# Chunked attention and two feed-forward layers on one core: seven block products on three PSUM banks per group, and another rule for GpSimd's share

## The chip, the cores and the metric

The kernel runs on one core of one Trainium2 chip. The engines are TensorE (PE, with its weight loads as PEld), VectorE (DVE), ScalarE (ACT), GpSimd (POOL) and SyncE (SP), which issues the DMAs. The metric is the time of one execution in microseconds, the median over runs on the device.

## The reference

Three steps follow each other on 3072 tokens (4 sequences of 768):

```python
# attention in chunks of 32 queries; 8 memory keys, 16 left, 8 right
a = softmax(q_c @ concat(mem_k, k_ctx).T / 8); out_c = a @ concat(mem_v, v_ctx)
x = out as (3072, 512)
h = np.maximum(x @ w_in, 0.0);  x = h * h @ w_out               # 512 -> 2048 -> 512
g = x @ w_gate;  silu = g * (1.0 / (1.0 + np.exp(-g)))
return (silu * (x @ w_val)) @ w_out2                            # 512 -> 1536 -> 512
```

Everything is float32 in and out. The weights come in as 64-bit words and are turned into float32 by the kernel itself.

## The kernel before

The tokens are six blocks of 512. Every matrix product is made of three products of high and low parts (`TERMS`), so each operand is split first: ACT writes the high part (`split`, line 414), DVE or POOL subtracts it to get the low part (line 421).

**First part.** Attention of all blocks and the first feed-forward layer of blocks 0 to 3 are done directly, with 2048 hidden columns in 16 steps (`first_layer`, line 668; `first_out`, line 696).

**Second part.** The last two blocks of the first layer and all three pairs of blocks of the second layer are done with 2-by-2 blocks and seven products in place of eight (the Strassen and Winograd scheme). A left side is a group of weights; its sums and differences are prepared by `sides` and kept in DRAM (L830, L379 to L402, L432 on `f` and `g` tiles), and come back by `load_in` or `load_out`. The right sides are sums of blocks of the activations, made and split by `rights` into tiles `r` and `x`. `group` (line 891) issues one product of 6 matmuls of 128x512 into a PSUM bank. `first_quad` runs seven products for each of 8 groups, and `second_gate` seven for each of 12 groups in each of three pairs, which makes 44 groups. After each product ACT copies the bank out (`copy`, line 441), or DVE adds it to a tile (`sub` on `FROM`, line 432); what is left is combined from tile to tile by `sub` with the costs `DIFF`, on DVE or POOL. `out_layer` (line 1001) does the way back in seven products over all groups, four times, each with two banks per product.

In a group the products come as 1, 5, 6, 2, 7, 3, 4. Product 2 is added onto the bank of 1 and product 3 onto that of 5, after ACT has copied those out; 6, 7 and 4 have a bank each, so a group uses five of the eight banks.

**The order.** Nothing of the order is written by hand. Each step is an `Op` with a cost for every engine that may do it, and `Plan.run` (a list scheduler) puts the ops on the engines in the order of their ranks; PE may look ahead over a few products. An op that DVE and POOL can both do goes to an engine only if the other would not end it sooner. The instructions are then issued in this fixed order, so each engine works through its own queue, and an instruction that waits holds up all that stand behind it. Pools of tiles: `PS` 8 banks, `T2` 5 tiles for what leaves the banks, `U` the blocks, `R` and `X` the split operands.

Of the kernel before, what the change touches and what calls it, by code (L numbers as in the profile page):

```python
# [39 lines left out]
HI, LO = 0, 1  # L40
# [10 lines left out]
QUAD = (1, 5, 6, 2, 7, 3, 4)  # L51
# [9 lines left out]
DUE = 12.0  # L61

# [11 lines left out]
class Op:  # L74
    __slots__ = (
        "engs", "fn", "deps", "succ", "bufs", "new", "n", "start", "end", "ready", "asap",
        "rank", "tail", "move", "eng", "soon", "at",
    )


class Plan:
# [9 lines left out]
    def op(self, engs, fn, reads=(), writes=(), tail=0.0, move=0.0):  # L91

        o = Op()
        o.engs, o.fn, o.tail, o.move, o.at = engs, fn, tail, move, self.due
        o.n, o.succ, o.start, o.eng, o.soon = len(self.ops), [], None, None, self.soon
# [57 lines left out]
    def run(self, pools, slack=12.0, ahead=8, phases=(), gives=None):  # L153
# [48 lines left out]
        def place(o, e):  # L202
# [6 lines left out]
            engines[e] = t + o.engs[e]  # L209
# [87 lines left out]
DIFF = {"DVE": 0.72, "POOL": 1.35}  # L297
# [7 lines left out]
def tile_chunked_attention_two_ffn(ctx: ExitStack, tc, qd, kd, vd, w1, w2, wo2, out):  # L305
# [45 lines left out]
    def words(src, token=None):  # L351
# [8 lines left out]
        def word(n):  # L360
# [17 lines left out]
            {"DVE": 0.5},  # L378
# [3 lines left out]
            (), (a,),  # L382
        )
        pl.op(
            {"DVE": 0.5},
# [4 lines left out]
            (), (a,),  # L390
        )
        pl.op(
            {"DVE": 0.8},
# [4 lines left out]
            (raw,), (a,),  # L398
        )
        pl.op(  # L400
            {"DVE": 0.8},
# [3 lines left out]
            (t,), (a,),  # L405
# [3 lines left out]
    def split(dst, src, reads, keys, n=512, diff=None):  # L409
# [9 lines left out]
        def low(e):  # L419
# [4 lines left out]
            costs, low, list(reads) + [(b, (q, HI)) for b, q in keys], [(b, (q, LO)) for b, q in keys]  # L424
        )

    def sub(out, x, y, op=ALU.subtract, engs=None):
# [5 lines left out]

        return pl.op(engs or DIFF, run, (x[0], y[0]), (out[0],))

# [9 lines left out]
    def whole(b):  # L445
        return (b, lambda: at(b))
# [17 lines left out]
    class Unit:  # L464
# [158 lines left out]
        def leave(self, xb, a):  # L623
# [6 lines left out]
                diff={"DVE": 0.69},  # L630
# [216 lines left out]
    def rights(b11, b12, b21, b22, name):  # L847
# [4 lines left out]
        yield 2, hilo(name, b21)  # L852
# [3 lines left out]
        sub(b11, b22, b11)  # L856
        yield 6, hilo(name, b11)
        sub(b21, b11, b21)
# [40 lines left out]
    FROM = {"DVE": 0.69}  # L899

    def first_quad(w, r):

        bank, pl.soon = {}, True
        a = pl.buf("T2", "a")
        b11, b12, b21, b22 = (pl.buf("U", n) for n in ("b11", "b12", "b21", "b22"))

        def product(i, onto=None):
            bank[i] = bank[onto] if onto else pl.buf("PS", f"p{i}")
            group(bank[i], w, i, r, onto is None)

        def squared(b):
            def run(e):
                if e == "ACT":
                    nc.scalar.activation(out=at(b), in_=at(b), func=AF.Relu)
                    nc.scalar.activation(out=at(b), in_=at(b), func=AF.Square)
# [349 lines left out]
```

## Time and profile before

| | |
|---|---|
| median of 3 runs | 1196.51 us (1194.54 to 1199.16) |
| profiled execution | 1196.86 us |
| its span, first to last instruction | 1194.8 us |
| PE busy | 1109.7 us (93%) |
| DVE busy | 994.5 us (83%), 1563 instructions |
| ACT busy | 604.6 us (51%), 1257 instructions |
| POOL busy | 473.9 us (40%), 353 instructions |
| mean granted TensorE clock | 0.977 of 2.4 GHz |

The profiled execution takes 2.1 us more than its span. Busy shares are averages over stages with different limits: the first 450 us hold the attention and the direct products, 463 to 612 us the eight groups of the first layer, and from about 612 us on the three pairs of the second layer follow. A time "for" another engine in a view of waits is the idle time that this engine's semaphore ended.

### The profile page before, as it was taken

What the parts mean: (1) busy time and instruction counts of PE and PEld (TensorE: products, weight loads), DVE (VectorE), ACT (ScalarE), POOL (GpSimd) and SP (SyncE); (2) the same over time, 40 slices, a digit from 0 to 9 for tenths busy, and PEclk for the clock granted to TensorE, in tenths of its full rate; (3) what the DMA queues carried; (4) which work ended last, traced back from release to release, by engine and by line L of the source; (5) the groups of instructions that cost most, each with busy time, mean ns of one, the idle gap of its engine ahead of it and who ended that gap; (6) DMA issues with size and microseconds to landing.
All of it is one profiled execution on the core that took longest, in us unless ns stands there. A gap on an engine that the chain in (4) does not pass through costs nothing.

```text
span 1194.8 us, 17679 instructions
## 1 busy us (share of the span) xinstructions
PE 1109.7 (93%) x6044; PEld 901.6 (75%) x6044; DVE 994.5 (83%) x1563; ACT 604.6 (51%) x1257; POOL 473.9 (40%) x353
## 2 busy tenths in 40 slices
PE   5898999999999997989799999669999999999998
PEld 5666788778877876868578887458888888888887
DVE  6999988888798886799997799998566998567992
ACT  5877756656656664556644344534122454223450
POOL 0324546666243344177822235881000571001640
PEclk9999999999999998999899999889999999999999
DMA  9664477778868688857599986665955365954462
GB/s 351 214 225 163 142 262 278 278 263 284 292 237 306 234 290 291 306 185 275 185 360 342 376 304 208 222 212 170 399 198 185 92 225 182 349 192 159 152 195 76
DMA packets 100073, 288.48 MB, mean 241 GB/s; under 512 B 10768, under 2 KB 14864, under 8 KB 99984
## 3 DMA queue, kind: packets, MB, share of 16 engines
q1 hardware_dynamic: 99984, 287.35, 68.7%
q8 instruction: 48, 0.79, 0.3%
q14 instruction: 41, 0.34, 0.1%
HBM read 210.24 MB, written 77.07 MB: 240 GB/s over the span
## 4 chain that ended last, share of the span: by engine, by line
PE 51%; DVE 24%; DMA 8%; issue 8%; ACT 5%; POOL 2%; SPq 0%; DVEq 0%; POOLq 0%; ACTq 0%
PE ps L891 28%; PE ps L1001 13%; PE ps L668 4%; PE ps L696 4%; DVE u L432 3%; DMA g<-in_w 3%; DVE g L421 3%; DVE a L568 3%; DVE r L421 3%; DVE f L394 2%; DVE f L432 2%; DVE t L432 1%; ACT t L524 1%; DVE f L402 1%; DVE f L379 1%
## 5 line engine op out<-in xcount | busy, mean ns | idle before, releaser
L891 PE MATMUL ps<-r,r 128*128 128x512 f32 x981 | 242.8, 390 | 3.8 <-ACT a L441 2.0
L891 PEld LDWEIGHTS ps<-r,r 128*128 128x128 f32 x981 | 184.4, 188 | 43.0 <-ACT a L441 2.4
L668 PE MATMUL ps<-x,r 128*128 128x512 f32 x768 | 190.0, 396 | 6.3 <-DVE r L421 4.4
L441 ACT ACTIVATE t<-ps 128x512 f32<-128x512 f32 x165 | 98.2, 596 | 153.3 <-PE ps L891 111.7
L668 PEld LDWEIGHTS ps<-x,r 128*128 128x128 f32 x768 | 142.2, 189 | 39.7 <-DVE r L421 5.6
L1001 PE MATMUL ps<-r,r 128*128 128x512 f32 x600 | 150.8, 402 | 17.4 <-ACT f L441 11.6
L891 PE MATMUL ps<-r,x 128*128 128x512 f32 x579 | 147.4, 394 | 5.7 <-ACT t L441 5.7
L1001 PEld LDWEIGHTS ps<-r,r 128*128 128x128 f32 x600 | 116.3, 195 | 44.5 <-ACT f L441 13.2
L696 PE MATMUL ps<-r,w 128*128 128x512 f32 x552 | 138.5, 401 | 12.0 <-POOL r L421 3.6
L696 PEld LDWEIGHTS ps<-r,w 128*128 128x128 f32 x552 | 104.9, 192 | 37.6 <-POOL w L421 4.0
L891 PEld LDWEIGHTS ps<-r,x 128*128 128x128 f32 x579 | 110.4, 191 | 29.8 <-ACT t L441 6.6
L414 ACT ACTIVATE g<-f 128x512 fp32r<-128x512 f32 (+1 forms) x136 | 76.9, 578 | 72.8 <-DVE f L394 26.7
L414 ACT ACTIVATE r<-u 128x512 fp32r<-128x512 f32 x126 | 75.2, 624 | 61.4 <-DVE u L432 29.1
L421 DVE TENSOR_TENSOR g<-f,g 128x512 fp32r<-128x512 f32 (+1 forms) x103 | 94.1, 923 | 7.9 <-ACT g L414 7.0
L421 POOL TENSOR_TENSOR r<-u,r 128x512 fp32r<-128x512 f32 x36 | 58.0, 1618 | 100.0 <-ACT r L414 87.4
L432 DVE TENSOR_TENSOR t<-t,ps 128x512 f32<-128x512 f32 x80 | 54.6, 683 | 48.1 <-PE ps L891 38.1
L421 POOL TENSOR_TENSOR r<-t,r 128x512 fp32r<-128x512 f32 x32 | 50.1, 1564 | 107.4 <-ACT r L414 99.7
L421 DVE TENSOR_TENSOR r<-u,r 128x512 fp32r<-128x512 f32 x90 | 79.6, 910 | 7.4 <-ACT r L414 6.6
L568 DVE STREAM_TRANSPOSE a<-t 32x128 f32<-32x128 f32 x256 | 77.4, 302 | 7.0 <-POOL t L552 2.8
L432 POOL TENSOR_TENSOR f<-f,f 128x256 f32<-128x256 f32 (+1 forms) x38 | 35.1, 924 | 113.0 <-DVE f L432 69.4
L432 POOL TENSOR_TENSOR u<-u,u 128x512 f32<-128x512 f32 x38 | 61.2, 1619 | 45.2 <-DVE u L432 22.1
L441 ACT ACTIVATE t<-t 128x512 f32<-128x512 f32 x36 | 22.7, 631 | 101.3 <-DVE t L432 101.3
(124 smaller groups left out, 2002.3 us busy)
## 6 DMA issues: line engine op xcount, KB each, us to landing
r<-tma SPq DMA_DIRECT2D x71, 512.0 KB, 5.2
g<-in_w SPq DMA_DIRECT2D x56, 512.0 KB, 4.8
r<-tmb SPq DMA_DIRECT2D x50, 512.0 KB, 3.6
x<-tma SPq DMA_DIRECT2D x37, 512.0 KB, 4.8
tma<-g SPq DMA_DIRECT2D x36, 512.0 KB, 3.7
tlb<-g SPq DMA_DIRECT2D x56, 256.0 KB, 3.4
tla<-g SPq DMA_DIRECT2D x24, 512.0 KB, 3.9
tmb<-g SPq DMA_DIRECT2D x42, 256.0 KB, 3.2
```

The source lines that it names most:

```text
L379: lambda: nc.vector.tensor_scalar(out=at(a), in0=at(a), scalar1=EXP_MIN, scalar2=EXP_MAX, op0=ALU.max, op1=ALU.min),
L394: lambda: nc.vector.scalar_tensor_tensor(out=at(a).bitcast(I32), in0=word(1), scalar=-0x40000000, in1=at(a).bitcast(I32), op0=ALU.bitwise_ ...
L402: lambda: nc.vector.tensor_tensor(out=at(a).bitcast(I32), in0=at(a).bitcast(I32), in1=at(t).bitcast(I32), op=ALU.add),
L414: lambda: nc.scalar.activation(out=dst(HI), in_=src(), func=AF.Copy),
L421: eng.tensor_tensor(out=dst(LO), in0=src(), in1=dst(HI).bitcast(F32), op=ALU.subtract)
L432: eng.tensor_tensor(out=out[1](), in0=x[1](), in1=y[1](), op=op)
L441: nc.scalar.activation(out=out[1](), in_=x[1](), func=func)
L568: nc.vector.transpose(out=o[g : g + 32, hh, :, :, m, :].rearrange("k s (f c) q -> k s f c q", c=2)[:, :, :, par, :], in_=a[r : r + 32, :, ...
L668: nc.tensor.matmul(at(hp), at(w)[:, 512 * a + k * P : 512 * a + (k + 1) * P], x[:, b, k, :], start=(n == 0), stop=(n == len(terms) - 1),)
L696: nc.tensor.matmul(at(accs[m]), at(w)[:, 512 * a + m * P : 512 * a + (m + 1) * P], at(h2)[:, 512 * b : 512 * b + 512], start=(i == 0 and n ...
L891: nc.tensor.matmul(at(bank), at(w[slot])[:, o : o + P], at(r[i, n])[:, 512 * b : 512 * b + 512], start=(first and n == 0 and m == 0), stop ...
L1001: nc.tensor.matmul(at(bank[i][n]), at(w[i][g // 2])[:, o : o + P], at(r)[:, 512 * b : 512 * b + 512], start=(first and m == 0), stop=(g == ...
```

## The change

The scheme of seven products is arranged in another way. Three banks serve a group: 1, 6, 7 and 4 are added one after the other onto the first, 5 and 3 onto the second, 2 has the third. The bank is read after each product, so what it holds is already a running sum, and tile-to-tile additions fall away. A new function `quads` issues the products: 1 and 5 of a group, then product 4 of the group before, then 6, 3, 2, 7. `out_layer` does the same with order 1, 5, 6, 3, 7, 2, 4. `rights` makes the same seven sums with one sign turned.

The scheduler has a new rule for POOL. Ops with all operands in SBUF are marked `shared`; if such an op starts on DVE while POOL is at work, its cost grows by `SLOWED` of the overlap. POOL takes an op only if it would be `AVOID` sooner than DVE. Some DVE costs are lowered to 0.45, 0.69 and 0.7.

```diff
+SLOWED, AVOID = 0.55, 0.3
...
-            engines[e] = t + o.engs[e]
+            cost = o.engs[e]
+            if e == "DVE" and o.shared:
+                cost += SLOWED * max(0.0, min(cost, engines["POOL"] - t))
+            engines[e] = t + cost
...
-                            x != e and busy(x, o.rank) + o.engs[x] < t + o.engs[e] for x in o.engs
+                            x != e and busy(x, o.rank) + o.engs[x] < t + o.engs[e] + (e == "POOL") * AVOID
+                            for x in o.engs
...
-DIFF = {"DVE": 0.72, "POOL": 1.35}
+DIFF = {"DVE": 0.69, "POOL": 1.3}
+FROM = {"DVE": 0.69}
...
+    def quads(lefts, r, begin):
+        last = None
+        for n, left in enumerate(lefts):
+            w, a, b, c = left(), *(pl.buf("PS", x) for x in "abc")
+            steps = begin(n)
+
+            def product(i, w=w, steps=steps, a=a, b=b, c=c):
+                bank = {1: a, 6: a, 7: a, 4: a, 5: b, 3: b, 2: c}[i]
+                pl.soon = True
+                group(bank, w, i, r, i in (1, 5, 2))
+                steps[i](bank)
+                pl.soon = False
+
+            product(1)
+            product(5)
+            if last:
+                last(4)
+            for i in (6, 3, 2, 7):
+                product(i)
+            last = product
+        last(4)
...
-    def second_gate(w, r):
...
-        product(6)
-        sub(whole(a), whole(a), whole(bank[6]), ALU.add, FROM)
-        product(2, 1)
-        copy(whole(d), whole(bank[1]), func=AF.Sigmoid)
-        sub(whole(d), whole(bank[1]), whole(d), ALU.mult, FROM)
-        product(7)
-        sub(whole(b), whole(a), whole(bank[7]), ALU.add, FROM)
-        sub(whole(c), whole(b), whole(c), ALU.add)
-        product(3, 5)
-        sub(whole(a), whole(a), whole(bank[5]), ALU.add, FROM)
-        copy(whole(e), whole(a), func=AF.Sigmoid, engs=C512)
-        sub(whole(e), whole(e), whole(a), ALU.mult)
-        sub(whole(c), whole(c), whole(e), ALU.mult)
-        product(4)
-        sub(whole(b), whole(b), whole(bank[4]), ALU.subtract, FROM)
-        sub(whole(b), whole(b), whole(d), ALU.mult)
...
+    def second_quads(left, r):
...
+            def third(k):
+                sub(whole(e), whole(e), whole(k), ALU.add, FROM)
+                copy(whole(f), whole(e), func=AF.Sigmoid, engs=C512)
+                sub(whole(f), whole(f), whole(e), ALU.mult)
+
+            def second(k):
+                sub(whole(a), whole(a), whole(k), ALU.add, FROM)
+                copy(whole(d), whole(a), func=AF.Sigmoid, engs=C512)
+                sub(whole(d), whole(d), whole(a), ALU.mult)
+
+            def seventh(k):
+                sub(whole(c), whole(k), whole(c), ALU.add, FROM)
+                sub(whole(c), whole(c), whole(f), ALU.mult)
+
+            return {
+                1: lambda k: copy(whole(a), whole(k)),
+                5: lambda k: copy(whole(c), whole(k)),
+                6: lambda k: copy(whole(e), whole(k)),
+                3: third, 2: second, 7: seventh,
+                4: lambda k: sub(whole(b), whole(k), whole(d), ALU.mult, FROM),
+            }
...
-        order = (1, 5, 2, 3, 7, 6, 4)
+        order = (1, 5, 6, 3, 7, 2, 4)
...
-                onto = {2: 1, 3: 5}.get(i)
+                onto = {6: 1, 7: 1, 4: 1, 3: 5}.get(i)
```

`first_quads` replaces `first_quad` in the same way. In all, the order has 1344 rows on DVE before and 1372 now, 1013 and 1062 on ACT, 358 and 220 on POOL, and 1358 on PE in both.

On PE, six products in a row inside a group of the second pair, before: product 1 on bank 112, then 5, 6, then 2 on 112 again, 7, and 3 on 5's bank 114 (an `r` or `x` behind the arrow is a split operand, the second one the left side).

```order
L891 MATMUL ps_112<-r_76,r_82 128x512 x3
L891 MATMUL ps_112<-x_86,r_82 128x512 x3
L891 MATMUL ps_114<-r_67,r_84 128x512 x3
L891 MATMUL ps_114<-r_79,r_84 128x512 x3
L891 MATMUL ps_115<-r_71,r_66 128x512 x3
L891 MATMUL ps_115<-x_87,r_66 128x512 x3
L891 MATMUL ps_112<-r_73,r_82 128x512 x3
L891 MATMUL ps_112<-r_74,r_82 128x512 x3
L891 MATMUL ps_113<-r_72,r_68 128x512 x3
L891 MATMUL ps_113<-x_87,r_68 128x512 x3
L891 MATMUL ps_114<-r_65,r_66 128x512 x3
L891 MATMUL ps_114<-r_63,r_66 128x512 x3
```

The same place now: products 1 and 5 on banks 113 and 116, product 4 of the group before on 117, then 6 on 113, 3 on 116 and 2 on 112.

```order
L902 MATMUL ps_113<-x_87,r_70 128x512 x3
L902 MATMUL ps_113<-r_82,r_70 128x512 x3
L902 MATMUL ps_116<-r_83,r_78 128x512 x3
L902 MATMUL ps_116<-r_69,r_78 128x512 x3
L902 MATMUL ps_117<-r_80,x_86 128x512 x3
L902 MATMUL ps_117<-x_87,x_86 128x512 x3
L902 MATMUL ps_113<-x_87,r_64 128x512 x3
L902 MATMUL ps_113<-r_79,r_64 128x512 x3
L902 MATMUL ps_116<-x_86,r_64 128x512 x3
L902 MATMUL ps_116<-r_76,r_64 128x512 x3
L902 MATMUL ps_112<-r_68,r_70 128x512 x3
L902 MATMUL ps_112<-r_65,r_70 128x512 x3
```

Four products of a group instead of two now wait until their bank has been read, each time with two other products between.

On DVE, all that one group of the second layer gives it when its part of the queue holds nothing else, before (`t` are T2 tiles, `u` and `a` blocks, `ps` banks):

```order
L432 TENSOR_TENSOR t_103<-t_103,ps_113 128x512
L432 TENSOR_TENSOR t_102<-ps_117,t_102 128x512
L432 TENSOR_TENSOR u_4556<-t_103,ps_119 128x512
L432 TENSOR_TENSOR a_93<-u_4556,a_93 128x512
L432 TENSOR_TENSOR t_103<-t_103,ps_116 128x512
L432 TENSOR_TENSOR u_4556<-u_4556,ps_118 128x512
L432 TENSOR_TENSOR t_105<-t_105,t_103 128x512
L432 TENSOR_TENSOR u_4556<-u_4556,t_102 128x512
L432 TENSOR_TENSOR a_93<-a_93,t_105 128x512
```

And now:

```order
L443 TENSOR_TENSOR t_103<-t_103,ps_118 128x512
L443 TENSOR_TENSOR t_101<-t_101,ps_115 128x512
L443 TENSOR_TENSOR t_104<-t_104,t_103 128x512
L443 TENSOR_TENSOR u_4502<-ps_119,u_4502 128x512
L443 TENSOR_TENSOR t_105<-t_105,t_101 128x512
L443 TENSOR_TENSOR u_4502<-u_4502,t_104 128x512
L443 TENSOR_TENSOR u_4512<-ps_119,t_105 128x512
```

Nine instructions are seven: one that reads a bank and one from tile to tile are gone.

On POOL, from the first row that combines tiles of a group of the first pair, before (`f` and `g` are tiles of the left sides' preparation):

```order
L432 TENSOR_TENSOR a_91<-a_91,t_101 128x512
L421 TENSOR_TENSOR g_88<-f_96,g_88 128x2x256
L432 TENSOR_TENSOR f_100<-f_97,f_100 128x256
L432 TENSOR_TENSOR t_102<-t_102,t_105 128x512
L432 TENSOR_TENSOR u_4573<-u_4573,t_104 128x512
L432 TENSOR_TENSOR a_93<-a_94,a_93 128x512
L432 TENSOR_TENSOR f_95<-f_96 128x256
L432 TENSOR_TENSOR f_96<-f_99,f_96 128x256
L432 TENSOR_TENSOR a_94<-a_94,t_102 128x512
L432 TENSOR_TENSOR t_105<-t_105,t_103 128x512
```

And now:

```order
L443 TENSOR_TENSOR t_105<-t_105,t_103 128x512
L443 TENSOR_TENSOR u_4514<-u_4514,t_104 128x512
L443 TENSOR_TENSOR f_95<-f_100 128x256
L443 TENSOR_TENSOR u_4516<-u_4516,t_105 128x512
L443 TENSOR_TENSOR t_102<-t_102,t_103 128x512
L443 TENSOR_TENSOR t_105<-t_105,t_101 128x512
L443 TENSOR_TENSOR t_103<-t_103,t_104 128x512
L443 TENSOR_TENSOR u_4521<-a_92,u_4521 128x512
L431 TENSOR_TENSOR x_87<-u_4512,x_87 128x512
L443 TENSOR_TENSOR u_4510<-a_93,u_4510 128x512
```

Of these ten rows, four belonged to the preparation of left sides; now one does, and the last three already sum or split hidden blocks for the way back.

## Rows read from the trace of the kernel before

**Rows 1.** Busy time by stretch; columns in the first line.

```profile
core 0: us, PE busy (x) PEld busy (x) DVE busy (x) ACT busy (x) POOL busy (x), PEclk, DMA share, GB/s
0.00:452.00 452.00, 417.46 (x3067) 335.48 (x3068) 391.90 (x783) 297.58 (x716) 196.28 (x172) 0.99 0.72 253
452.00:840.00 388.00, 342.13 (x1438) 277.24 (x1437) 346.13 (x438) 189.98 (x338) 189.26 (x127) 0.94 0.76 267
840.00:1195.00 355.00, 350.08 (x1542) 288.89 (x1541) 256.46 (x344) 117.01 (x204) 88.32 (x55) 1.00 0.58 199
```

**Rows 2.** PE's waits from 452 to 840 us: total, times, longest.

```profile
PE ps L891 <- ACT t L441: 15.6, 4, 9.6
PE ps L1001 <- ACT f L441: 11.1, 2, 6.8
...
PE ps L891 <- ACT a L441: 2.0, 1, 2.0
PE ps L891 <- DVE t L432: 1.8, 1, 1.8
```

**Rows 3.** Busy time by stretch, three pieces of 452 to 840 and before.

```profile
440.00:460.00 20.00, 15.86 (x69) 12.46 (x67) 20.00 (x25) 11.46 (x22) 13.06 (x8) 0.98 0.69 248
520.00:612.00 92.00, 76.95 (x313) 61.01 (x311) 91.66 (x97) 54.65 (x99) 65.61 (x42) 0.91 0.69 239
730.00:804.00 74.00, 51.41 (x206) 40.17 (x204) 73.86 (x75) 32.16 (x60) 61.35 (x40) 0.88 0.61 204
```

**Rows 4.** Timeline around PE's longest wait: start us, us, engine, line, [idle before].

```profile
754.80 1.52 PE L891 MATMUL ps<-x,r 128*128 128x512 f32 x6
...
763.16 0.63 ACT L414 ACTIVATE g<-f 128x512 fp32r<-128x512 f32 x1 [1.68 <-DVE f L394]
...
765.26 0.57 ACT L441 ACTIVATE t<-ps 128x512 f32<-128x512 f32 x1
...
765.89 1.65 PE L891 MATMUL ps<-x,r 128*128 128x512 f32 x3 [9.57 <-ACT t L441]
```

**Rows 5.** Timeline of all engines, 750 to 757 us: DVE beside POOL.

```profile
750.76 3.18 POOL L432 TENSOR_TENSOR a<-a,a 128x512 f32<-128x512 f32 x2
...
752.70 0.67 DVE L432 TENSOR_TENSOR t<-t,ps 128x512 f32<-128x512 f32 x1
...
754.12 1.59 POOL L432 TENSOR_TENSOR t<-t,t 128x512 f32<-128x512 f32 x1 [0.18 <-ACT t L441]
...
754.47 1.78 DVE L394 SCALAR_TENSOR_TENSOR f<-g,f 128x512 int32<-128x512 int32 x1
```

**Rows 6.** Timeline of DVE, 455 to 458 us, with POOL idle.

```profile
455.78 0.41 DVE L432 TENSOR_TENSOR f<-f 128x256 f32<-128x256 f32 x1
456.12 0.41 DVE L386 TENSOR_SCALAR f<-f 128x512 int32<-128x512 int32 x1
...
457.06 0.68 DVE L394 SCALAR_TENSOR_TENSOR f<-g,f 128x512 int32<-128x512 int32 x1
457.66 0.68 DVE L421 TENSOR_TENSOR r<-a,r 128x512 fp32r<-128x512 f32 x1
```

**Rows 7.** Groups of instructions by line, 452 to 840 us, shapes apart: busy, mean.

```profile
L379 DVE TENSOR_SCALAR f<-f 128x512 f32<-128x512 f32 x22 | 13.5, 614 | 1.1 <-ACT f L366 1.1
...
L432 DVE TENSOR_TENSOR f<-f,f 128x256 f32<-128x256 f32 x12 | 10.8, 902 | 0.0
```

**Rows 8.** Chain of waits: time of one product of 6 matmuls.

```profile
636.41 1.36 PE ps L891 x6
637.77 1.36 PE ps L1001 x6
```

**Rows 9.** Costliest groups, part 5 of the page.

```profile
L441 ACT ACTIVATE t<-ps 128x512 f32<-128x512 f32 x165 | 98.2, 596 | 153.3 <-PE ps L891 111.7
...
L432 DVE TENSOR_TENSOR t<-t,ps 128x512 f32<-128x512 f32 x80 | 54.6, 683 | 48.1 <-PE ps L891 38.1
```

**Rows 10.** PE's waits from 840 us to the end, all of them.

```profile
PE ps L1001 <- ACT f L441: 0.9, 2, 0.5
```

**Rows 11.** PE's waits up to 452 us, the longest two.

```profile
PE ps L615 <- DVE a L568: 9.1, 11, 2.1
PE ps L486 <- DMA s<-in_k: 6.9, 3, 5.7
```

More of the change, by code (lines that the diff above doesn't have):

```diff
@@ L77 @@
         "rank", "tail", "move", "eng", "soon", "at",
+        "shared",
     )
@@ L423, in split @@
         pl.op(
-            costs, low, list(reads) + [(b, (q, HI)) for b, q in keys], [(b, (q, LO)) for b, q in keys]
+            costs, low, list(reads) + [(b, (q, HI)) for b, q in keys], [(b, (q, LO)) for b, q in keys],
+            shared=diff is not FROM,
         )
@@ L897, in group @@
         pl.op({"PE": 1.375}, run, (w[slot], r[i, 0], r[i, 1]), (bank,), tail=0.2)
[L899 to L915, printed above, removed]
-                else:
-                    nc.vector.scalar_tensor_tensor(
-                        out=at(b), in0=at(b), scalar=0.0, in1=at(b), op0=ALU.max, op1=ALU.mult
-                    )
-            pl.op({"ACT": 1.26, "DVE": 0.75}, run, (), (b,))
-        product(1)
-        copy(whole(a), whole(bank[1]))
-        product(5)
-        copy(whole(b22), whole(bank[5]))
-        product(6)
-        sub(whole(a), whole(a), whole(bank[6]), ALU.add, FROM)
-        product(2, 1)
-        copy(whole(b11), whole(bank[1]), func=AF.Relu)
-        copy(whole(b11), whole(b11), func=AF.Square)
-        product(7)
-        sub(whole(b21), whole(a), whole(bank[7]), ALU.add, FROM)
-        sub(whole(b22), whole(b21), whole(b22), ALU.add)
-        squared(b22)
-        product(3, 5)
-        sub(whole(b12), whole(a), whole(bank[5]), ALU.add, FROM)
-        squared(b12)
-        product(4)
-        sub(whole(b21), whole(b21), whole(bank[4]), ALU.subtract, FROM)
-        squared(b21)
-        pl.soon = False
-        return b11, b12, b21, b22
@@ new lines, in first_quads, with begin, squared, run @@
+    def first_quads(left, r):
+        got = []
+        def begin(n):
+            a = pl.buf("T2", "a")
+            b11, b12, b21, b22 = blocks = [pl.buf("U", x) for x in ("b11", "b12", "b21", "b22")]
+            got.append(blocks)
+            def squared(b):
+                def run(e):
+                    if e == "ACT":
+                        nc.scalar.activation(out=at(b), in_=at(b), func=AF.Relu)
+                        nc.scalar.activation(out=at(b), in_=at(b), func=AF.Square)
+                    else:
+                        nc.vector.scalar_tensor_tensor(
+                            out=at(b), in0=at(b), scalar=0.0, in1=at(b), op0=ALU.max, op1=ALU.mult
+                        )
+                pl.op({"ACT": 1.26, "DVE": 0.75}, run, (), (b,), shared=True)
+            def third(k):
+                sub(whole(b12), whole(b12), whole(k), ALU.add, FROM)
+                squared(b12)
+            def second(k):
+                sub(whole(b11), whole(a), whole(k), ALU.add, FROM)
+                squared(b11)
+            def seventh(k):
+                sub(whole(b22), whole(k), whole(b22), ALU.add, FROM)
+                squared(b22)
+            def fourth(k):
+                copy(whole(b21), whole(k), func=AF.Relu)
+                copy(whole(b21), whole(b21), func=AF.Square)
+            return {
+                1: lambda k: copy(whole(a), whole(k)),
+                5: lambda k: copy(whole(b22), whole(k)),
+                6: lambda k: copy(whole(b12), whole(k)),
+                3: third, 2: second, 7: seventh, 4: fourth,
+            }
+        quads([lambda q=q: left.load_in(q) for q in range(NF1 // 2)], r, begin)
+        return got
@@ L994, in out_layer @@
             assert got == i
-            first = g == 0 and i not in (2, 3)
+            first = g == 0 and i in (1, 5, 2)
             def run(i=i, g=g, r=r, first=first):
```

99 lines of the change are left out of this document (44 added, 55 removed).

## The prediction

> **What bounds the kernel now.** I read the busy time by stretch first. From 840 us on PE is busy for 350.1 of 355.0 us at the full granted clock of 1.00, and does 1542 matmuls, 0.227 us each [rows 1]. All its waits there add up to 0.9 us [rows 10]. This third of the kernel is bound by its matmuls, whose number the change leaves alone, so nothing can be gained there but nothing covers a new wait either. From 452 to 840 us it looks different: 1438 matmuls at 0.227 us are 326 us of work, and the stretch takes 388 [rows 1]. 62 us are lost: 388.0 - 342.1 = 45.9 us with PE idle, and some 16 us in which it was busy at a low clock (mean 0.94 of 2.4 GHz). Up to 452 us PE is idle for another 34.5 us [rows 1], a part of it for the first loads (6.9 us) and for transposes on DVE (9.1 us) [rows 11].
>
> Who holds PE up in the middle stretch? Nearly all of the long waits are for ACT's copies out of the banks, 15.6 and 11.1 us of them [rows 2]. But ACT is busy for only 190 of 388 us [rows 1]. The timeline shows what lies behind it: PE ended a product at 756.3, and the next had to wait until 765.9 for a copy that takes 0.57 us. ACT's queue stood still ahead of this copy, because the instruction in front needed a DVE result from the preparation of left sides [rows 4]. So DVE is the cause, one queue further on. In three pieces of the stretch, 186 us in all, DVE is busy for 20.0 of 20, 91.7 of 92 and 73.9 of 74 us, and PE's clock falls to 0.91 and 0.88 in the long ones [rows 3].
>
> Why is DVE full there? With POOL idle, a full-length instruction starts 0.60 us after the one before and a short one (256 columns, or one operand) 0.34 us [rows 6]. While POOL works on SBUF tiles, DVE's instruction on SBUF tiles does not get through: one takes 1.78 us, while one that reads a bank takes its usual 0.67 us beside POOL [rows 5]. In the middle stretch 83 of DVE's 438 instructions are short (five groups, the first and the last of them in [rows 7], at means of 614 and 902 ns instead of some 410). Undisturbed, 83 x 0.34 + 355 x 0.60 = 241 us would do; DVE was busy for 346 [rows 1]. The 105 us above that belong to 127 POOL instructions of 1.49 us each [rows 1], 0.83 us of DVE's time apiece. POOL costs DVE more than the 0.60 us that DVE would need to do the work itself.
>
> **The change, part by part.** The sum is made against the profiled execution, 1196.9 us (span 1194.8 and 2.1 around it); the median of the runs is 0.4 us lower.
>
> *Fewer additions.* Each of the 44 groups loses one instruction that reads a bank and one from tile to tile, and each `out_layer` two of both. In the middle stretch lie 20 groups and two of these layers: 24 of each kind. The first kind takes DVE 24 x 0.60 = 14 us; the second is on DVE or POOL, counted next.
>
> *POOL's share.* POOL's order falls from 358 to 220 rows. In the middle stretch I put 127 instructions down to about 70: 57 fewer, of which 24 vanish with the scheme and 33 go to DVE, 33 x 0.57 = 19 us. At 0.83 us each the 57 give back 47 us. DVE's load goes from 346 to 346 - 14 + 19 - 47 = 304 us, below PE's 326. In the three full pieces lie 140 of POOL's 189 us [rows 1, 3], 74%, so 0.74 x 47 = 35 us come back there, less half of the 5 us that the first two numbers leave: 32. The pieces then take 154 us in place of 186. Their 588 matmuls need 133 us, so the whole of it can be used. The refund in low clock is in this, since it is elapsed time that is counted. **-32 us.**
>
> *The first 452 us.* POOL has 172 instructions there [rows 1] and its order becomes about a third shorter up to the same place. Of PE's 34.5 us of idle time only part hangs on DVE, the rest on loads and on the start. I take **-3 us**; bounds are +6 (as much the other way as the shift of a few preparations can do) and -12 (a third of the idle time).
>
> *More handoffs.* Each group now has four products that add onto a bank just read, instead of two. Two products lie between, 2 x 1.36 = 2.7 us [rows 8], and the reader needs 0.60 us on ACT or 0.68 on DVE [rows 9]. Where queues are clear, that is free: 24 groups with two such handoffs each ran after 840 us without a wait on them [rows 10]. Where they are not, the 20 groups of the middle stretch had 40 handoffs, and the waits of L891 for ACT and DVE were 15.6 + 2.0 + 1.8 = 19.4 us [rows 2], 0.49 us each. Forty more cost between 0 and 19.4 us and its low clock; DVE being relieved, I stay near zero: **+3 us.**
>
> *One more copy on ACT* per group and two per `out_layer`, 52 x 0.60 = 31 us in all, 14 of them in the middle stretch: ACT has 198 us free there [rows 1]. Nothing, unless the queue stands still, which is the case above. *From 840 us on and the tail*: nothing, as PE has no wait to give back, and the last product is followed by one copy where one subtraction stood.
>
> Sum: -32 - 3 + 3 = -32. 1196.9 - 32 - 0.4 = **1164.5**, say 1165 us.
>
> **The rivals.** *DVE stops mattering.* If the order now follows the engines so well that PE never waits in the middle stretch, all 62 us come back: 1196.5 - 62 - 3 = 1131. For it: DVE's load drops below PE's. Against: 304 us in 326 leaves little slack, and the preparation of left sides comes in bursts at its due times.
>
> *The relief lands off the path.* PE's longest wait came from a chain of small instructions, ACT to DVE and back [rows 4]. These are not fewer, and those which leave POOL now stand in DVE's queue, ahead of the reads. If the chain is no shorter, only the small terms stay: about -4, 1192, no change that a measurement shows. For it: DVE's rows grow by 28 although 52 bank reads fell away. Against: the links of that chain are the very instructions that took 1.5 to 1.8 us beside POOL.
>
> *The handoffs become the bound; slower.* The place is the groups from 463 to 612 us and from 730 us on. A product must find its bank read 2.7 us later, and this now holds for four of seven. If DVE's bursts still delay reads by more than that, the 62 us stay, 40 more handoffs cost 0.49 us each, 19.6, and low clock adds its 16/46 of that, 7: 1196.5 + 27 = 1223. It decides when a reader stands more than two products behind. For it: ACT's queue stood still for 9 us before [rows 4], and fewer banks let PE run less far ahead. Against: after 840 us the same handoff cost nothing.
>
> What idle gaps do to the clock stands in [rows 3]: 0.88 in the piece with most of them, 1.00 where there are none [rows 1]. The Trainium skill (TensorE: Matmul & The Clock Gate, section "A second HAM failure mode: psum-queue depth-cycling") reports a kernel that cycled through banks, idled briefly between groups of matmuls, and swung between its two clock levels while the single matmul looked as long as ever. By that rule short waits at 88 new handoffs would cost clock also after 840 us, and this rival with its 1223 us would be the likeliest, against 1165 by the rows; the trace before, with two handoffs a group and a clock of 1.00 there, does not bear it out.
>
> **Chances.** Forecast (1145 to 1185) 0.55; all back 0.12; off the path 0.17; handoffs 0.13; the rest 0.03, with the case that DVE's long instructions are not POOL's doing (then 14 - 19 make it 1202). A measurement can tell about 0.5%, 6 us. Faster than that: the forecast, all back, and a little of the third, 0.72. Same 0.14, slower 0.14. The range reaches from 1140, between the forecast's lower end and the full refund, to 1200, which takes in "off the path" and leaves out the handoffs.
>
> **What would show it.** Right: POOL near 70 instructions in the stretch of the first-layer groups and the first pair; DVE's full-length SBUF instructions near 0.7 to 0.8 us in the mean instead of about 1; the long waits of PE for ACT in that place down from 27 us to under 10; clock of the whole above 0.985; nothing changed in the last two pairs. Wrong: waits of L902 (the new `group`) for ACT or DVE of one to three microseconds in all groups, the last two pairs too; DVE still without a gap for tens of microseconds while PE waits; or T2 tiles, of which a group now uses four out of five, holding ACT's copies back.

## The result, and the profile after

The changed kernel takes **1151.5 us** in the median of 4 runs (1146.5 to 1152.4), the kernel before 1195.5 in the same comparison: ratio 0.962, 95% interval 0.958 to 0.966, so 44 us less. It was forecast at 1165 us; the direction was right, 13.5 us were missing, and the range held the time. The profiled execution is the fastest of the four, 1146.5 us with a span of 1144.8, 50.0 less than the span before. So times taken from the traces show about 6 us more gain than the medians do.

The page of the changed kernel: busy time of the engines, then the granted clock in 40 slices, then the shares of the chain.

```profile
PE 1098.2 (96%) x6044; PEld 894.2 (78%) x6044; DVE 922.9 (81%) x1595; ACT 636.7 (56%) x1308; POOL 287.4 (25%) x215
...
PEclk9999999999999999999999999899999999999999
...
PE 65%; DVE 21%; ACT 5%; issue 4%; DMA 4%; SPq 0%; DVEq 0%; ACTq 0%
```

POOL's work fell from 474 to 287 us and DVE's from 995 to 923, though DVE now has 32 instructions more in the trace. The clock over all is 0.994 (0.977 before).

To see where the 50 us came from, I cut both traces at the same places of the program: the first product of the groups, and the end of the first pair. Busy time by stretch, columns as in [rows 1], the kernel before:

```profile
0.00:469.60 469.60, 428.00 (x3104) 343.50 (x3105) 404.71 (x800) 304.63 (x729) 206.83 (x177) 0.99 0.72 254
469.60:853.00 383.40, 344.60 (x1459) 279.97 (x1458) 337.84 (x427) 184.72 (x328) 180.01 (x122) 0.95 0.76 271
853.00:1194.80 341.80, 337.08 (x1485) 278.15 (x1483) 251.94 (x337) 115.22 (x201) 87.02 (x54) 1.00 0.57 191
```

And the changed kernel:

```profile
0.00:446.60 446.60, 420.43 (x3092) 338.06 (x3093) 404.99 (x835) 305.75 (x729) 149.06 (x128) 1.00 0.76 264
446.60:803.00 356.40, 339.80 (x1465) 276.99 (x1464) 304.29 (x435) 196.72 (x351) 122.80 (x78) 0.98 0.83 293
803.00:1144.70 341.70, 337.95 (x1490) 279.12 (x1488) 213.59 (x326) 134.22 (x230) 15.49 (x10) 1.00 0.59 194
```

**23.0 us came from the first part, 27.0 from the groups up to the end of the first pair, nothing from the last two pairs.** The border is not quite fair: ahead of the first group lie 3104 matmuls before and 3092 now. Twelve of the direct products, 2.7 us at 0.227 us each, now come behind it and count in the middle. In the middle, DVE did 8 instructions more in 33.5 us less, and POOL 44 fewer. PE's waits of that stretch in the changed kernel (what waited, for whom, total, times, longest), which answer to [rows 2]:

```profile
PE ps L902 <- ACT t L452: 6.5, 4, 2.9
PE ps L1039 <- DVE a L443: 5.5, 1, 5.5
PE ps L902 <- DVE a L443: 3.2, 2, 2.6
PE ps L902 <- DVE u L443: 1.2, 2, 1.0
PE ps L1039 <- ACT f L452: 0.2, 1, 0.2
```

The waits for ACT, 26.7 us in the first two lines of [rows 2], are 6.7 now. After 803 us the view lists no wait of PE at all, where [rows 10] had 0.9 us.

Of the 23 us of the first part, half lies just ahead of the groups. PE in the kernel before (start, us, [idle before]):

```profile
452.40 2.91 PE L696 MATMUL ps<-r,w 128*128 128x512 f32 x12
458.76 0.56 PE L696 MATMUL ps<-r,w 128*128 128x512 f32 x1 [3.45 <-ACT r L414]
462.93 6.90 PE L696 MATMUL ps<-r,w 128*128 128x512 f32 x23 [3.62 <-POOL r L421]
469.67 1.52 PE L891 MATMUL ps<-r,r 128*128 128x512 f32 x6
```

The same place in the changed kernel:

```profile
441.11 5.66 PE L707 MATMUL ps<-r,w 128*128 128x512 f32 x24
446.61 1.52 PE L902 MATMUL ps<-r,r 128*128 128x512 f32 x6
```

The last direct products begin 11.3 us earlier (441.1 for 452.4), and from there to the first group it takes 5.5 us instead of 17.3, another 11.8. Of these, 7.1 are the two waits, 2.7 are the 12 matmuls that now come later, and the other 2 or so are the low clock around the waits (0.80 from 452.4 to 469.7 us, 1.00 now). What PE waited for was the last hidden block. On DVE, before it, stood this (three of six such rows in a row):

```profile
448.28 1.79 DVE L421 TENSOR_TENSOR r<-a,r 128x512 fp32r<-128x512 f32 x1
450.00 1.78 DVE L421 TENSOR_TENSOR r<-t,r 128x512 fp32r<-128x512 f32 x1
451.70 1.79 DVE L421 TENSOR_TENSOR g<-f,g 128x512 fp32r<-128x512 f32 x1
```

And on POOL:

```profile
449.49 5.15 POOL L421 TENSOR_TENSOR r<-a,r 128x512 fp32r<-128x512 f32 x3
458.78 4.09 POOL L421 TENSOR_TENSOR r<-t,r 128x512 fp32r<-128x512 f32 x1 [4.14 <-ACT r L414]
462.84 1.46 POOL L421 TENSOR_TENSOR r<-a,r 128x512 fp32r<-128x512 f32 x1
```

Two engines that each take 1.7 to 1.8 us per instruction do in 10 us what DVE alone would do in 7 (an estimate, 12 x 0.60). And the delay seems to go both ways: the split that PE waited for took POOL 4.09 us, while DVE went on with the undisturbed run of which [rows 6] shows a part; the one right after it took 1.46.

DVE's groups in the middle stretch of the changed kernel (line, names, shapes, count | busy, mean ns | idle before):

```profile
L431 DVE TENSOR_TENSOR r<-u,r 128x512 fp32r<-128x512 f32 x49 | 33.7, 719 | 2.1 <-ACT r L424 2.1
L431 DVE TENSOR_TENSOR g<-f,g 128x512 fp32r<-128x512 f32 x32 | 30.9, 976 | 1.7 <-ACT g L424 1.4
...
L404 DVE SCALAR_TENSOR_TENSOR f<-g,f 128x512 int32<-128x512 int32 x20 | 17.5, 887 | 0.0
...
L443 DVE TENSOR_TENSOR u<-u,u 128x512 f32<-128x512 f32 x25 | 16.9, 704 | 0.0
L443 DVE TENSOR_TENSOR f<-f,f 128x256 f32<-128x256 f32 x21 | 16.2, 772 | 0.1
```

Before, from 452 to 840 us:

```profile
L421 DVE TENSOR_TENSOR r<-u,r 128x512 fp32r<-128x512 f32 x48 | 46.7, 997 | 5.8 <-ACT r L414 5.1 <-PE ps L1001 0.7
L421 DVE TENSOR_TENSOR g<-f,g 128x512 fp32r<-128x512 f32 x31 | 35.0, 1135 | 1.5 <-ACT g L414 1.3
L432 DVE TENSOR_TENSOR u<-u,u 128x512 f32<-128x512 f32 x34 | 34.7, 1034 | 0.3
```

The hidden blocks' splits and sums went from about 1.0 us to 0.70 to 0.72, near the undisturbed 0.68. The preparation of left sides (`g<-f,g`, `f<-g,f`, and `f<-f,f`, 902 in [rows 7]) is still disturbed; POOL has 78 instructions left in this stretch.

### The profile page after: what moved, and what is told of

Same layout as the page of the kernel before. It is cut to its first block, busy times and chain, and to the rows that moved or that the text cites. A ratio compares the mean times of both kernels' runs of the same rounds, so it can differ in the third digit from the quotient of the medians.

```text
span 1144.8 us, 17421 instructions
## 1 busy us (share of the span) xinstructions
PE 1098.2 (96%) x6044; PEld 894.2 (78%) x6044; DVE 922.9 (81%) x1595; ACT 636.7 (56%) x1308; POOL 287.4 (25%) x215
## 4 chain that ended last, share of the span: by engine, by line
PE 65%; DVE 21%; ACT 5%; issue 4%; DMA 4%; SPq 0%; DVEq 0%; ACTq 0%
PE ps L902 30%; PE ps L1039 19%; PE ps L707 8%; PE ps L679 7%; DVE g L431 4%; DVE a L579 3%; DMA g<-in_w 3%; DVE f L443 2%; DVE f L404 2%; DVE f L412 2%; DVE f L389 1%; PE ps L497 1%; DVE r L431 1%; PE ps L626 1%; ACT t L535 1%
## 5 line engine op out<-in xcount | busy, mean ns | idle before, releaser
L902 PE MATMUL ps<-r,r 128*128 128x512 f32 x990 | 249.6, 392 | 7.1 <-ACT t L452 3.6
L902 PEld LDWEIGHTS ps<-r,r 128*128 128x128 f32 x990 | 186.8, 189 | 48.4 <-ACT t L452 4.9
L679 PE MATMUL ps<-x,r 128*128 128x512 f32 x768 | 189.3, 395 | 3.9 <-DVE r L431 2.9
L679 PEld LDWEIGHTS ps<-x,r 128*128 128x128 f32 x768 | 141.4, 188 | 37.0 <-DVE r L431 5.4
L707 PE MATMUL ps<-r,w 128*128 128x512 f32 x540 | 132.7, 394 | 4.2 <-DVE w L431 4.2
L707 PEld LDWEIGHTS ps<-r,w 128*128 128x128 f32 x540 | 100.5, 188 | 28.3 <-DVE w L431 6.7
L902 PE MATMUL ps<-r,x 128*128 128x512 f32 x426 | 108.3, 393 | 3.8 <-ACT t L452 2.9
L443 DVE TENSOR_TENSOR t<-t,ps 128x512 f32<-128x512 f32 x72 | 49.4, 685 | 70.0 <-PE ps L902 69.9
L431 DVE TENSOR_TENSOR g<-f,g 128x512 fp32r<-128x512 f32 (+1 forms) x120 | 99.1, 838 | 5.5 <-ACT g L424 4.6
L902 PEld LDWEIGHTS ps<-r,x 128*128 128x128 f32 x426 | 80.2, 189 | 21.9 <-ACT t L452 3.3
L902 PE MATMUL ps<-x,r 128*128 128x512 f32 x336 | 91.8, 390 | 0.0
L452 ACT ACTIVATE t<-t 128x512 f32<-128x512 f32 x72 | 45.4, 631 | 65.1 <-DVE t L443 64.2
L431 DVE TENSOR_TENSOR r<-u,r 128x512 fp32r<-128x512 f32 x104 | 71.7, 716 | 11.7 <-ACT r L424 11.7
L902 PEld LDWEIGHTS ps<-x,r 128*128 128x128 f32 x336 | 63.5, 189 | 13.4
L1039 PE MATMUL ps<-x,r 128*128 128x512 f32 x252 | 63.9, 393 | 5.7 <-DVE a L443 5.5
```

Of the source, the lines that this page charges most:

```text
L431: eng.tensor_tensor(out=dst(LO), in0=src(), in1=dst(HI).bitcast(F32), op=ALU.subtract)
L443: eng.tensor_tensor(out=out[1](), in0=x[1](), in1=y[1](), op=op)
L452: nc.scalar.activation(out=out[1](), in_=x[1](), func=func)
L679: nc.tensor.matmul(at(hp), at(w)[:, 512 * a + k * P : 512 * a + (k + 1) * P], x[:, b, k, :], start=(n == 0), stop=(n == len(terms) - 1),)
L707: nc.tensor.matmul(at(accs[m]), at(w)[:, 512 * a + m * P : 512 * a + (m + 1) * P], at(h2)[:, 512 * b : 512 * b + 512], start=(i == 0 and n ...
L902: nc.tensor.matmul(at(bank), at(w[slot])[:, o : o + P], at(r[i, n])[:, 512 * b : 512 * b + 512], start=(first and n == 0 and m == 0), stop ...
```

## The experiments

My theory: each POOL instruction on SBUF tiles costs DVE at least as much time as DVE would need to do it, DVE's lateness is what PE waits for, and most of the gain comes from POOL's smaller share. The rivals: that the new scheme brings it (fewer additions); that the handoffs on three banks take some of it back; that it is one lucky order. All ratios are to the kernel before, with 95% intervals. Times of the stretches, in us, are those of the profiled execution: up to the first product of the groups; from there to the end of the first pair; the rest. The last column counts POOL's instructions.

| version | us | ratio | first / middle / rest | POOL in the middle |
|---|---|---|---|---|
| before | 1195.5 | 1 | 469.7 / 383.5 / 341.6 | 122 |
| changed | 1151.5 | 0.962 (0.958 to 0.966) | 446.6 / 356.3 / 341.9 | 78 |
| e1 rule and costs only | 1169.6 | 0.978 (0.975 to 0.981) | 452.3 / 373.5 / 340.1 | 81 |
| e2 scheme only | 1189.3 | 0.995 (0.993 to 0.997) | 458.5 / 386.9 / 341.0 | 113 |
| e3 before, order shuffled | 1184.9 | 0.991 (0.988 to 0.994) | 467.0 / 374.3 / 343.0 | 122 |
| e4 before, without POOL | 1178.7 | 0.986 (0.983 to 0.988) | 491.4 / 342.1 / 344.1 | 0 |
| e5 changed, without POOL | 1149.3 | 0.960 (0.958 to 0.962) | 470.4 / 336.7 / 341.8 | 0 |
| e6 changed, POOL early only | 1131.7 | 0.945 (0.944 to 0.947) | 450.7 / 338.8 / 341.8 | 1 |
| e7 changed, 160 POOL reads more | 1173.0 | 0.979 (0.978 to 0.981) | 449.6 / 379.6 / 341.9 | 238 |
| e8 changed, 340 POOL writes more | 1163.9 | 0.972 (0.971 to 0.974) | 448.6 / 369.6 / 341.9 | 418 |
| e9 changed, one product between | 1157.2 | 0.968 (0.966 to 0.970) | 449.9 / 363.6 / 341.9 | 77 |
| e10 costs only | 1201.4 | 1.005 (1.003 to 1.007) | 475.2 / 375.4 / 349.0 | 118 |
| e11 changed, order shuffled | 1146.6 | 0.958 (0.955 to 0.961) | 454.1 / 352.9 / 341.9 | 63 |
| e12 before, POOL early only | 1147.8 | 0.960 (0.957 to 0.964) | 459.6 / 350.0 / 341.4 | 0 |

The stretches do not hold the same work in every version. With the new scheme 12 matmuls of the direct products always come behind the first group, with the old one none, and the middle holds 1459 matmuls before, 1465 in the changed kernel, 1482 in e2 and 1441 in e4. Against the kernel before, up to 5 us of a difference in the middle is work that has only moved.

### The parts alone: e1, e10 and e2

e1 gives the kernel before the rule and the costs, e10 the costs alone; e2 is the new scheme with the old rule and costs.

```diff
+SLOWED, AVOID = 0.55, 0.3      # e1; in e10 and e2: 0.0, 0.0
...
-DIFF = {"DVE": 0.72, "POOL": 1.35}
+DIFF = {"DVE": 0.69, "POOL": 1.3}    # e1, e10
...
```

> The kernel before with the new rule for POOL and the new costs alone; the scheme of seven products stays. POOL's order has 239 rows in place of 358, DVE's 1451 in place of 1344. Theory (POOL's instructions block DVE's): 119 fewer at 0.83 us of DVE's time each give 99 us back, 107 more DVE instructions at 0.57 us take 61, so 38 us less load on DVE, most of it where DVE is the bound: 1165 to 1178 us. Rival 1 (the scheme does it, with its shorter chains): 1188 us or more. Rival 2 (any new order of the list scheduler moves the time): anywhere, with waits at other places.

> The changed kernel with the old rule for POOL and the old costs: the new scheme alone. POOL's order has 330 rows, DVE's 1276. Theory: 28 fewer on POOL give 23 us back and 68 fewer on DVE 39 us, 62 us in all over the kernel, about half of it where DVE is the bound: 1165 to 1180 us. Rival 1: 1150 to 1158, nearly the whole gain. Rival 3 (the tighter handoffs cost something that the rule hides): 1190 us or more, with waits of the products for ACT.

> The kernel before with the lower DVE and POOL costs alone (0.45, 0.69 and 0.7 on DVE, 1.3 on POOL), without the rule for POOL (SLOWED and AVOID both 0). If the rule is what brought the rule-only version to 1170: about as before, 1184 to 1200, since other orders of the same work differed by about 10 us. If the costs, through another order, brought it: 1165 to 1178, with the first group at 450 to 455 us and POOL still at over 400 us of work.

e1 came out as expected, 1169.6. e10 is no faster than before (1201.4, just above its range), so the costs alone bring nothing and the rule for POOL, on top of them, brings the whole of e1: 32 us from e10 to e1. By the profiled executions it is 34, of which 23 lie in the first part and only 2 in the middle (10 against the kernel before). The two numbers of the rule, `SLOWED` and `AVOID`, were not tried apart. e2 missed: the scheme alone gives 6 us. In the middle it takes 386.9 us for 383.5, with 23 matmuls more, so at equal work it gives some 2 us there. The first part is 11.2 us shorter, of which 2.7 are the 12 matmuls moved; most of the rest is the stall ahead of the groups, where PE waits for 1.5 us in e2 instead of 7.1 (another 1.9 come just behind the first group). The scheme did lighten DVE, 337.8 to 321.8 us in the middle, and PE still waits. In e2, from the first group on:

```profile
PE ps L902 <- DVE u L443: 17.4, 6, 8.1
PE ps L1039 <- ACT f L452: 7.8, 2, 5.9
PE ps L902 <- ACT t L452: 5.2, 2, 4.0
```

With POOL's old share the relief lands off the path, and waits for DVE's readers of banks come up. With POOL's share cut the same scheme is worth 18.1 us (1169.6 to 1151.5); by the profiled executions 21, of which 17 lie in the middle stretch. The rule and the costs are worth 26 us alone and 38 on top of the scheme (1189.3 to 1151.5). In the middle each part alone does little, 2 to 10 us, and both together 27. An order alone can move that stretch by 9 us (e3), so the small numbers are rough.

### Without POOL: e4 and e5

Both forbid POOL what DVE can do as well (POOL takes an op only if it would be 1000 us sooner, in e5 by way of `AVOID`).

> The kernel before with POOL never chosen for an elementwise op: 13 rows on POOL, 1672 on DVE. Theory: 328 more DVE instructions at 0.57 us are 187 us, and the time lost beside POOL, about 190 us over the kernel, is gone: DVE's load hardly changes, and the time is 1185 to 1205 us. If POOL's help were worth its own time, 328 instructions of 1.3 to 1.6 us, the load on DVE would be 187 us higher and the time 1250 us or more.

> The changed kernel with POOL never chosen for an elementwise op: DVE's order has 1570 rows in place of 1372. Without POOL the kernel before lost 22 us up to the first group and won 41 between there and the end of the first pair. Theory: the same two signs here, the first part 30 to 45 us longer than in the changed kernel, the groups and the first pair 10 to 25 us shorter: 1165 to 1185 us in all. If the new rule had already found the best share everywhere, both parts would be longer: 1190 us or more.

Both ranges were too high, by 6 and 16 us. **The kernel before is 17 us faster when POOL does not help at all.** Its middle stretch goes from 383.5 to 342.1 us (4 of these because 18 matmuls come later), while the first part gets 21.7 us longer; in the changed kernel the middle gains 19.6 and the first part loses 23.8. In the middle, POOL's help is a loss; up to the groups it is worth some 20 us. Why it helps there is not settled: without POOL, DVE is busy for 409.0 us in the first part against 405.0 with it, no fuller, but in the changed kernel without POOL (e5) PE's clock falls to 0.91 to 0.95 between 180 and 360 us, where it is 1.00 with it. The two versions without POOL differ by 29 us: the scheme, with the new costs, is worth more there than in any other pair, and 18 us of it lie in the first part at equal work.

### POOL early only: e6 and e12

From the first product of a group on, POOL gets no more of this work; e6 on the changed kernel, e12 on the kernel before with rule and costs.

```diff
+            self.late = self.late or ("PE" in o.engs and o.soon)
...
-    ... + (e == "POOL") * AVOID
+    ... + (e == "POOL") * (1000.0 if self.late else AVOID)
```

> The changed kernel with the rule kept until the scheduler has placed the first product of the first group, and POOL not chosen for any elementwise op after that: POOL's order has 133 rows in place of 220, DVE's 1458 in place of 1372. Theory: the first part as in the changed kernel (first group at about 447 us), the 356 us to the end of the first pair down to 332 to 346: 1125 to 1142 us. Rival (DVE needs POOL's help there): 1155 us or more.

> The kernel before with the rule for POOL and its costs, and with no elementwise work on POOL from the first product of the groups on: the old scheme of five banks with the treatment of POOL that gave 1132 with the new scheme. Theory: from the first group to the end of the first pair it takes what the kernel before without POOL took there, 342 us, and the first group starts at 450 to 467 us, the rest takes 342: 1136 to 1153. The difference to 1132 is then the whole worth of the new scheme, 5 to 20 us. Rival, that with all work on DVE the two additions per group which the new scheme saves decide (48 x 0.65 = 31 us in the middle): 1163 or more, with DVE full from 452 to 800 us.

Both as expected. **e6 takes 1131.7 us and beats both kernels.** Its three costliest groups on DVE in the middle stretch:

```profile
L433 DVE TENSOR_TENSOR r<-u,r 128x512 fp32r<-128x512 f32 x67 | 44.3, 686 | 2.9 <-ACT r L426 2.9
L445 DVE TENSOR_TENSOR u<-u,u 128x512 f32<-128x512 f32 x42 | 28.1, 686 | 0.0
L433 DVE TENSOR_TENSOR g<-f,g 128x512 fp32r<-128x512 f32 x34 | 23.0, 686 | 3.9 <-ACT g L426 3.8
```

Its waits of PE, from the first group to the end of the kernel:

```profile
PE ps L1041 <- DVE x L433: 2.2, 1, 2.2
PE ps L904 <- ACT t L454: 0.7, 1, 0.7
PE ps L1041 <- DVE r L433: 0.2, 1, 0.2
```

Every one of these groups now has the undisturbed mean, and so have all the others of this stretch with two inputs of 128x512 (680 to 692 ns). Busy time in e6's middle stretch (columns as in [rows 1]):

```profile
450.70:789.50 338.80, 335.62 (x1464) 275.07 (x1463) 290.06 (x510) 196.12 (x349) 1.56 (x1) 0.99 0.86 307
```

DVE does 75 instructions more than in the changed kernel (510 for 435), in 14.2 us less. At 290.06 / 510 = 0.569 us each, the 75 are worth 42.7 us, so 77 POOL instructions had cost DVE 42.7 + 14.2 = 56.9 us, 0.74 each, more than it takes DVE to do them. The old scheme gives nearly the same price. The middle stretch of e1:

```profile
452.30:825.70 373.40, 341.00 (x1458) 278.29 (x1457) 330.63 (x470) 186.20 (x329) 119.63 (x81) 0.96 0.79 282
```

And of e12:

```profile
459.60:809.60 350.00, 336.98 (x1452) 274.26 (x1451) 303.63 (x539) 189.09 (x333) 0.00 (x0) 0.99 0.84 297
```

69 more in 27.0 us less: (69 x 0.563 + 27.0) / 81 = 0.81 us. Before against e4 gives 0.78 in the same way.

The difference of e12 and e6, 16.1 us, is what the scheme is worth once POOL is out of the middle; by the traces it is 19.7, at equal work 14 in the middle and 6 ahead of the groups. And e12, the old scheme, is as fast as the whole change (their intervals overlap).

### The block itself: e7 and e8

Useless work on POOL in the changed kernel, beside the first-layer groups and the first pair: e7 multiplies a 128x128 tile, which nothing needs any more there, by itself 160 times, e8 only writes it, 340 times.

```diff
+            nc.gpsimd.tensor_tensor(out=ident, in0=ident, in1=ident, op=ALU.mult)   # e7, 8 at a time
+            nc.gpsimd.memset(ident, 0.0)                                            # e8, 17 at a time
```

> The changed kernel, all orders kept, with 8 small useless POOL products of 128x128 on one SBUF tile after each of the 20 groups of the first layer and of the first pair, 160 in all, some 70 us of POOL's time. Theory (POOL reading SBUF blocks DVE): DVE's instructions on SBUF tiles grow longer in that stretch and PE waits for them; 1165 to 1200 us. Rival (what costs is POOL's own lateness, not a block): as long as the next kernel.

> The same places with 17 POOL memsets of the same tile each, which write SBUF and read nothing, about as much of POOL's time. Theory, if the block comes from POOL's reads: DVE's instructions keep their length, 1146 to 1158 us. If any work of POOL on SBUF blocks DVE: as slow as the kernel with the reads.

Groups of instructions in e7's middle stretch, the added work on POOL and the low parts of the left sides on DVE:

```profile
L924 POOL TENSOR_TENSOR ident<-ident 128x128 f32<-128x128 f32 x160 | 88.8, 555 | 11.3
...
L431 DVE TENSOR_TENSOR g<-f,g 128x512 fp32r<-128x512 f32 x32 | 35.4, 1117 | 1.1 <-DMA r<-tma 1.1
```

The same two in e8:

```profile
L924 POOL MEMSET ident<- 128x128 f32 x340 | 72.0, 212 | 18.6
...
L431 DVE TENSOR_TENSOR g<-f,g 128x512 fp32r<-128x512 f32 x32 | 29.9, 946 | 1.9 <-DMA r<-tma 1.1 <-ACT g L424 0.7
```

The mean of that DVE group, 976 ns in the changed kernel, is 1117 beside more reads and 946 beside more writes. With the same 435 instructions DVE is busy for 317.0 us in e7's middle stretch and 297.8 in e8's (304.3 in the changed kernel). So the reads lengthen DVE's work and these writes don't. The Trainium skill (SBUF — State Buffer, section "Who interferes with whom") says the same: a DVE instruction with two SBUF inputs is in the way of a GpSimd instruction that reads SBUF, not of one that only writes. But e8 missed its range: it lost 12 us though DVE was not lengthened. What shows is that DVE waits for POOL's own results, in e8's view of waits:

```profile
DVE f L443 <- POOL f L443: 8.0, 3, 4.3
```

That these explain the 12 us is inferred. So e7's 21.5 us are not the price of blocking alone. And the smaller instruction costs less: a 128x128 product cost DVE (317.0 - 297.8) / 160 = 0.12 us, a usual 128x512 instruction 0.74 to 0.81.

### The handoffs: e9

Product 4 stands behind 7 of its own group, with no weaving by hand.

```diff
-            product(1)
-            product(5)
-            if last:
-                last(4)
-            for i in (6, 3, 2, 7):
+            for i in (1, 5, 6, 3, 2, 7, 4):
                 product(i)
-            last = product
-        last(4)
```

> The changed kernel with product 4 put behind product 7 of its own group and no weaving by hand (1, 5, 6, 3, 2, 7, 4, then the next group). The scheduler's look-ahead still puts something between: 56 of the additions onto a bank just read have one product between them and the one before on that bank, where the changed kernel has two nearly everywhere (143 with two, 2 with one). One product is 1.36 us, a reader takes 0.60 to 0.68 us. If a handoff is no more than reader plus passing on, a wait is under 0.3 us and 56 of them cost 0 to 17 us: 1150 to 1168, and the waits of L902 for ACT and DVE after the first pair are short and many, or none. If the interleaving is what carries the change (each handoff then costs 0.5 us and its low clock): 56 x 0.5 x 1.35 = 38 us or more, 1185 and above, with the last two pairs longer by 15 us or more.

As the first theory expected: 1157.2. The last two pairs, where more than half of the additions with one product between lie, take 341.9 us as in the changed kernel, and the view of waits lists none of PE there, so a reader on a clear queue fits behind a single product. What is lost, 5.7 us by the medians and 10.6 by the profiled executions, is lost earlier: 3.3 of the 10.6 in the first part, where the edit does nothing, and 7.3 in the middle.

### The order alone: e3 and e11

One constant of the scheduler, which sets how late some steps may come, is changed from 0.12 to 0.13; no work is added or removed.

> The kernel before with one planning number moved (the latency between engines 0.13 in place of 0.12), so that the scheduler writes another order for the same work; 350 rows on POOL, 1342 on DVE. Theory: 1188 to 1204 us. Rival 2 (order luck): off by more than 15 us either way, which would make a share of the gain an accident.

> The changed kernel with one number of the scheduler changed (LATE 0.13 for 0.12), which shuffles the order and removes nothing: how far does the order alone move the changed kernel? The kernel before moved by 10.5 us. Theory: the gain of 44 us is that of the work and not of one lucky order: 1138 to 1163. If it is mainly a lucky order: 1170 to 1190.

e3 came out 10.5 us faster, 3 below the range, e11 4.9 us faster than the change. Differences of 5 to 10 us between two versions of this kernel can be the order's alone: the 6 us of e2, and e9's, are of that size, and so are the 8 us between the middle stretches of e4 and e12. The 44 us of the change are not: three orders of the old work took 1184.9 to 1201.4 us (before, e3, e10), three of the new 1146.6 to 1157.2 (changed, e9, e11).

## Why the prediction was right, and where it fell short

**What bounds the kernel, and why.** Right. The price of a POOL instruction, worked out as 0.83 us from [rows 1] and [rows 6], is 0.74 to 0.81 by three pairs of kernels that differ in POOL's share. DVE's load in the middle stretch was to fall by 42 us. The same work in both, from the last direct products to the end of the first pair, in the kernel before:

```profile
452.40:853.40 401.00, 355.13 (x1495) 288.00 (x1494) 350.65 (x445) 191.38 (x340) 190.15 (x128) 0.94 0.77 272
```

And in the changed kernel:

```profile
441.10:803.10 362.00, 345.40 (x1489) 281.58 (x1488) 309.79 (x441) 200.56 (x357) 126.09 (x81) 0.98 0.83 294
```

DVE's load fell by 40.9 us.

**Fewer additions and POOL's share: right in kind, too small.** With the handoffs this was to bring 29 us, and the two lines show 39, by executions that differ by 6 us more than the medians. Three of the ten between are the handoffs; the rest is the refund: 32 of DVE's 42 us were to come back as time, and by the traces 39 of 41 did. The 74% that this rests on, POOL's share in the three full pieces [rows 3], was itself a little too high, since 12 of the 20 us of the first piece lie ahead of 452 us; the right share would have made the term 2 us smaller still. What the share of an average missed is the stall at 452 to 470 us: it gave back all of its 7.1 us of waits and some 2 us of low clock. Either part of the change alone does away with most of it (0.7 us of waits are left there in e1, 1.5 in e2). The shares of scheme and POOL were not separated in the sum, and they do not add: in the middle each alone is worth 2 to 10 us, both together 27. POOL was put at about 70 instructions and had 78.

**The first 452 us: the step that failed most.** It was taken at -3 with bounds of +6 and -12, on the ground that only part of PE's idle time hung on DVE. By the last direct products it was -11.3, just inside the bounds and nearly four times the term. The same work is 9.6 us earlier in e1, which has only the rule and the costs, 5.7 later in e10, which has only the costs, and 1.5 earlier in e2, which has only the scheme. So it is mostly the rule that did it. Some of the 11.3 is luck of the order: with the order shuffled (e11) the place comes at 448.6 us instead of 441.1. PE's wait for the transposes on DVE [rows 11], 9.1 us, is 3.7 in the changed kernel, which is about half of the gain:

```profile
PE ps L626 <- DVE a L579: 3.7, 4, 1.0
```

**More handoffs, +3.** They cost nothing that can be seen: no wait after 803 us, with four additions onto a read bank per group. In the middle L902 waited for 10.9 us, against 19.4 of L891 [rows 2]. Two products are longer than a reader, as the reason said; in e9 one was enough. The 9 us for which ACT's queue was said to have stood still [rows 4] are too many: of the time from 756.3 to 765.3 us ACT waited for DVE for 4.7 (3.03 and 1.68) and was at work for the rest. **ACT's copies and the last two pairs, 0:** right, 341.7 for 341.8 us.

**The rivals.** "DVE stops mattering" (1131) was not this change, but it is e6: with POOL's work out of the middle that stretch takes 338.8 us, PE busy for 335.6, and the time is 1131.7. The number fits better than its parts: 7 us came ahead of the last direct products and 56 behind them, by the traces, where the rival had 3 and 62. "Off the path" is nearly what e2 did in its middle stretch. "The handoffs become the bound" (1223) did not come, neither here nor in e9; in e2 the waits of L902 rose to 26.2 us from 19.4, a third of the price it was given. The rule that spoke against the change, the Trainium skill's on banks in turn (TensorE: Matmul & The Clock Gate, section "A second HAM failure mode: psum-queue depth-cycling"), finds no case here: the granted clock is 1.00 after 803 us and 0.98 in the middle, up from 0.95.

**What was not weighed.** The prediction computed that POOL cost DVE more than it saved, and yet asked only what the change would leave of it, not whether the rest was still a loss. It was, by another 20 us.

## What to carry to other kernels

Before giving elementwise work to GpSimd to relieve VectorE, compare DVE's means beside a busy and an idle POOL, multiply the excess by POOL's instructions, and set that against the time that DVE would need to do the work itself. Where DVE is the late engine and the operands are in SBUF, leaving POOL idle can be the gain; try it stage by stage, since it was a loss here in one stage and a help in another. And judge a rearrangement only after such a block is gone: the same scheme was worth 6 us with POOL's old share, and 16 to 29 once that was cut or gone.

## What was not expected of the hardware

POOL's instructions are lengthened as well as DVE's. A split took it 4.09 us in the stall above and the next one 1.46; that it was DVE that held it up is inferred from what ran beside it. In the middle stretch of the changed kernel these sums of POOL's have means of 1.8 and 2.1 us:

```profile
L443 POOL TENSOR_TENSOR u<-u,u 128x512 f32<-128x512 f32 x15 | 27.3, 1835 | 43.0 <-DVE r L431 23.5 <-DMA a<-yd 19.4
...
L443 POOL TENSOR_TENSOR u<-a,u 128x512 f32<-128x512 f32 x7 | 15.0, 2141 | 16.0 <-DVE a L443 11.0 <-DVE u L443 4.9
```

One-input instructions of DVE are lengthened too, not only those with two inputs, as the 614 ns in [rows 7] let one guess: `f<-f` 128x512 of int32 has a mean of 688 ns in the changed kernel (L396) and, in e6 with POOL idle, 421 (L398). The changed kernel:

```profile
L396 DVE TENSOR_SCALAR f<-f 128x512 int32<-128x512 int32 x20 | 13.6, 688 | 0.1
```

And e6:

```profile
L398 DVE TENSOR_SCALAR f<-f 128x512 int32<-128x512 int32 x20 | 8.3, 421 | 0.0
```

The 340 writes of 128x128 on POOL lengthened nothing on DVE in sum (297.8 us for 304.3).
